# Pooled attention and a shrink MLP on one core: other PSUM banks for two pairs, one turn by DMA, the keys turned a block later, the last stores on two queues

## The chip, the core and the metric

The kernel runs on one core of a Trainium2 chip. The core has five engines that run side by side, each with its own in-order instruction stream: TensorE (PE, matrix products into PSUM), VectorE (DVE) and ScalarE (ACT) for element-wise work, GpSimd (POOL), and SyncE (SP), which here only issues DMAs. They meet through semaphores alone. The metric is the device time of one execution in microseconds (us); four executions of the kernel before gave a median of 294.24 us (293.37 to 294.52).

## The reference

Inputs are q, k and v of shape (8 batches, 8 heads, 576 tokens, 64), and two weight matrices.

```python
k_p = k.reshape(B, H, Sp, 8, D).mean(axis=3)          # 72 pooled keys a head
v_p = v.reshape(B, H, Sp, 8, D).mean(axis=3)
attn = softmax(q @ k_p.T / sqrt(D))
x = (attn @ v_p) -> (4608 tokens, 512)
h = x @ w_in                                          # 512 -> 2048
g = h - tanh(h)
out = g @ w_out                                       # 2048 -> 512, float32
```

## The kernel before, in words

**Two tilings overlap.** Attention works on batches of 576 tokens, in four blocks of 128 tokens and a fifth of 64 (block 4). The MLP works on nine groups of 512 tokens (TG = 512). Group 1, tokens 512 to 1023, thus needs block 4 of batch 0, blocks 0 to 2 of batch 1 and half of block 3 of batch 1. The rest of block 3 and block 4 of batch 1 belong to group 2. The attention result of a block lies in SBUF as x_sb (tokens on the partitions) and must be turned into xT (features on the partitions) before the MLP can use it. `x_pe_transpose` (lines 468 to 482) turns a block on PE: four matmuls with the identity into one PSUM bank, then one ACT copy into xT. `x_dma_transpose` (lines 457 to 466) turns it by a transposing DMA, issued by SP. The list `late` holds blocks that are turned by DMA once a group's pairs are done.

**Every order is written out by hand**, and each engine runs its instructions in the order of the program text. PSUM has eight banks of 128 x 512 floats, addressed by number. In the stretch that matters, `ps_any` hands out banks 5, 6, 7 in rotation, whatever asks for one. A bank that comes round again is free only when the engine that reads it has finished.

**The stretch around the change** is the output half of group 0 and the start of group 1. The loop over u = 0..15 runs `mlp_o` sixteen times, four matmuls of 512 columns each (line 540): quarter qd = u // 4 of the hidden units, token tile tb = u % 4. The four token tiles accumulate in banks 3, 4, 2 and 0, and are copied out to O in the last quarter (u = 12 to 15): tiles 0 and 2 by ACT, tiles 1 and 3 by DVE (line 549), and then stored by SP. Between these `mlp_o` calls stands the attention of batch 1: pooling of its keys (on POOL, lines 248 to 258), the turn of the keys (`k_transpose`, line 312; two banks, which DVE copies to KB at lines 302, 303 and 306), the turns of q (line 217, one bank each, copied by ACT), scores and their exponentials, and per block `av` (two banks, read by DVE, lines 415 and 416, into x_sb) with its turn (line 475, one bank, copied by ACT at line 482). Three banks per block, and three in the rotation: each turn uses the bank of the turn before it.

**Groups 1 to 8** run seven `h_pair`s and two `h_one`s (lines 558 to 576). A pair makes two hidden blocks in two neighbouring banks; ACT takes the tanh of both (line 570), DVE subtracts it (line 571) and thereby frees the banks. The bank list is (0, 2, 4, 6, 0, 2, 4), and the two ones use banks 0 and 1. In group 1 alone DVE also makes sums of weights (`w_sum`, line 597): two fp16 operands in SBUF, one sum after each of the first four pairs. Before the first pair it makes the larger sum `w_sum(b12, ...)`. At the same time POOL pools the values of batch 2 (`pool_v`, lines 269 to 293). Then come seven products per group (line 614), with the scores and `av` of the next batch in between. The last group is group 8; its last product is stored by ACT and SP (line 1026), after stores from SP and POOL (line 631).

Of the kernel before, what the change touches and what calls it, by code (L numbers as in the profile page):

```python
# [42 lines left out]
def kernel(  # L43
# [9 lines left out]
    nc = tc.nc  # L53
# [184 lines left out]
    def halves(n, b):  # L238
        return ((0, n),) if b < 2 else ((0, n // 2), (n // 2, n))

    def pool_k(b, eng, t0=0, t1=NT, mid=(), dep=None):
        r = k_raw[b % 2].rearrange("p t (j d) -> p t j d", d=D)[:, t0:t1, :, :]
        if b not in kdups:
            kdups[b] = work.tile([128, NT, 2, D], BF16, name="kd", tag="kd")
        kd = kdups[b][:, t0:t1, :, :]
        n = t1 - t0
        for ta, tb in halves(n, b):
            first = eng.tensor_tensor(  # L248
                out=r[:, ta:tb, 0:4, :], in0=r[:, ta:tb, 0:4, :], in1=r[:, ta:tb, 4:8, :], op=ALU.add
            )  # L250
            if dep is not None and ta == 0:
                after([first], dep)
        for c in mid:
            load_w2(c)
        eng.tensor_tensor(  # L255
            out=r[:, :, 0:2, :], in0=r[:, :, 0:2, :], in1=r[:, :, 2:4, :], op=ALU.add
        )
        eng.tensor_tensor(  # L258
            out=kd,
            in0=r[:, :, 0:1, :].to_broadcast([128, n, 2, D]),  # L260
            in1=r[:, :, 1:2, :].to_broadcast([128, n, 2, D]),
            op=ALU.add,
        )
        return first
# [158 lines left out]
    def new_x():  # L423
        return work.tile([128, 2, 4, D], BF16, name="x_sb", tag="x_sb", bufs=5)
# [16 lines left out]
    def av(b, blk, alloc, by_dma):  # L441
        x_sb = new_x()
        if by_dma:
            av_both(b, blk, x_sb)
        else:
            for half in range(2):
                av_half(b, blk, half, x_sb, alloc)
        if by_dma:
            if b * S + blk * 128 < (b + 1) * TG:
                x_dma_transpose(b, blk, x_sb)  # L450
            else:
                late.append((b, blk, x_sb))
        return x_sb

    late = []
# [78 lines left out]
    def mlp_o(g, tb, i0, i1, gts, pool=None):  # L534
        if i0 == 0:
            p, tag = pool or (ps_o, "o_ps")
            o_tiles[tb] = p.tile([128, DM], FP32, name="o_ps", tag=tag)
        o_ps = o_tiles[tb]
        for i in range(i0, i1):
            nc.tensor.matmul(  # L540
                o_ps[:, :],
                lhsT=gts[i][:, tb * 128 : (tb + 1) * 128],
                rhs=w2b[:, i, :],
                start=(i == 0),
                stop=(i == NHID - 1),
            )
        if i1 == NHID:
            o_sb = O[:, tb, :]
            (nc.vector.tensor_copy if g == 0 and tb % 2 else nc.scalar.copy)(
                out=o_sb, in_=o_ps[:, :]  # L550
            )
            for r0, r1, dst in out_segments(g * TG + tb * 128, 128):
                nc.sync.dma_start(out=dst, in_=o_sb[r0:r1, :])
# [12 lines left out]
    def h_pair(g, p, b0, ts):  # L566
        h_mms(g, p, PS[:, b0, :])
        h_mms(g, p + NP, PS[:, b0 + 1, :])
        t2 = TS[:, 2 * ts : 2 * ts + 2, :]
        nc.scalar.activation(out=t2, in_=PS[:, b0 : b0 + 2, :], func=ACT.Tanh)  # L570
        nc.vector.tensor_sub(out=Gt[:, p, :, :], in0=PS[:, b0 : b0 + 2, :], in1=t2)  # L571
# [129 lines left out]
    def after(lds, dep):  # L701
        for ld in lds:
            tc.add_manual_dep(
                ld.ins,
                dep.ins.name,
                mybir.DependencyInfo(mybir.DependencyClass.Sync, mybir.DependencyReason.DATA),
            )
# [212 lines left out]
    pend = []  # L920
    for u in range(16):
        qd, tb = u // 4, u % 4
        mlp_o(0, tb, qd * 4, qd * 4 + 4, gts, o_pools[tb])
        if u == 0:
            q_cast(1, nc.scalar.copy, 2)
            load_q(2)
        if u == 2:
            k_transpose(1, ps_any, (nc.vector.tensor_copy, nc.vector.tensor_copy))
        if u == 3:
            q_pe_transpose(1, (0, 1), "act")  # L930
        if u == 4:
            q_pe_transpose(1, (2,), "act")
            w_sum(w2s[:, 1, :, :], b11, b12, ALU.add)
            v1_done = pool_v(1, nc.vector)
            after(
                [
                    w_sum(w2s[:, 3, :, :], b21, b11, ALU.subtract, nc.gpsimd, k, k + 2)
                    for k in range(0, NP, 2)
                ],
                v1_done,  # L940
            )
        if u == 5:
            q_pe_transpose(1, (3,), "act")
        if 4 <= u <= 8:
            scores_wide(1, (u - 4,))
        if u == 6:
            q_pe_tail(1)
        if u == 8:
            scores_tail(1)
        if u in (9, 11):  # L950
            n = (u - 9) // 2
            nc.scalar.mul(
                out=w2s[:, 4, 4 * n : 4 * n + 4, :], in_=b22[:, 4 * n : 4 * n + 4, :], mul=-1.0
            )
        if u >= 9:
            if u >= 11 and pend:
                x_pe_transpose(1, *pend.pop(0))
            if u <= 13:
                pend.append((u - 9, av(1, u - 9, ps_any, False)))
    pool_k(2, nc.gpsimd)  # L960
    pool_v(2, nc.gpsimd)
    w_sum(b12, b22, b12, ALU.subtract)

    for g in range(1, NG):
        nb = g + 1 if g + 1 < B else None
        nn = g + 2 if g + 2 < B else None
        for p in range(NP - 1):
            c = p if g > 1 else p - 1
            if nb is not None and 0 <= c < 3:
                q_cast_part(nb, c)  # L970
            h_pair(g, p, (0, 2, 4, 6, 0, 2, 4)[p], p % 2)
            if g == 1 and p < 4:
                w_sum(w2s[:, 0, :, :], b11, b22, ALU.add, k0=2 * p, k1=2 * p + 2)
            if 3 <= p < 6:
                sum_p(2 * p - 6, 2 * p - 4)
            if nb is not None and p == 0:
                k_dma_transpose(nb)
            if g > 1 and p == 0:
                for tb in (2, 3, 0, 1):
                    store_tile(g - 1, tb)  # L980
            if nb is not None and p == 0:
                k_place(nb, nc.gpsimd.tensor_copy)
            if nb is not None and 0 <= c < 3:
                q_dma_transpose(nb, 2 * c, min(2 * c + 2, R + 1))
            if nb is not None and c == 2:
                if nn is not None:
                    load_k(nn)
                    load_v(nn)
                    load_q(nn)
        h_one(g, NP - 1, 1, 0, 2)  # L990
        h_one(g, NP - 1, 0, 1, 3)
        sum_p(6, 8)
        sum_q(0, 4)
        sum_q(4, 8)
        while late:
            x_dma_transpose(*late.pop(0))
        ps_a = Banks(2, 3, 4, 5, 0, 1)
        for u in range(14):
            n, half = u // 2, u % 2
            bk, lhs, rhs = products[n]  # L1000
            if n == 6 and g == NG - 1:
                break
            product(g, bk, lhs, rhs, 4 * half, 4 * half + 4, n < 2)
            if half:
                after_product(g, n)
                if g == 1 and n in (1, 2):
                    w_sum(w2s[:, 2, :, :], b21, b22, ALU.add, k0=4 * n - 4, k1=4 * n)
            if nb is not None:
                if u < NT:
                    scores(nb, u)  # L1010
                if u == NT:
                    ps_a.n += 2
                if u in (6, 7, 8, 9, 11):
                    av(nb, (6, 7, 8, 9, 11).index(u), ps_b1, True)
                if u == 6 and nn is not None:
                    pool_k(nn, nc.gpsimd, dep=gate[0])
                    pool_v(nn, nc.gpsimd)
        if g < NG - 1:
            nc.scalar.copy(out=O[:, 0:2, 0:HD], in_=chain(g, C1))  # L1019
    store(NG - 1, 1, (nc.sync, nc.gpsimd), HD, DM)  # L1020
    bk, lhs, rhs = products[6]
    for tt, eng in ((0, nc.scalar.copy), (1, nc.vector.tensor_copy)):
        product(NG - 1, bk, lhs, rhs, 0, NP, False, (tt,))
        eng(out=O[:, tt, 0:HD], in_=part(NG - 1, C1, tt))
        for n, (r0, r1, dst) in enumerate(out_segments((NG - 1) * TG + tt * 128, 128)):
            (nc.scalar if tt == 0 or n else nc.sync).dma_start(
                out=dst[:, 0:HD], in_=O[r0:r1, tt, 0:HD]
            )

# [29 lines left out]
```

## Time and profile before

| what | us |
|---|---|
| median of four runs | 294.24 |
| the profiled execution, whole | 294.93 |
| its span, first to last instruction | 293.2 |
| PE busy in the span | 278.6 |
| DVE busy in the span | 222.9 |
| PE idle before the key turn, at 37.18 | 0.59 |
| PE idle before group 1's first matmul, at 54.99 | 0.67 |
| PE idle before group 1's first single block, at 67.92 | 0.58 |
| PE idle at the starts of groups 3, 4, 5 | 0.92, 0.52, 0.76 |

The clock of PE was granted at 0.997 of full speed on average. Times in the text count from the start of the span. A line of the timeline gives start, duration, engine, source line, operation, output and inputs, their shapes, and in brackets how long the engine had been idle and what released it. An instruction's duration includes what it waits for after it was dispatched; POOL's are rough. The chain of waits is followed back from the last instruction, at each step to what released it.

### The profile page before, as it was taken

What the parts mean: (1) busy time and instruction counts of PE and PEld (TensorE: products, weight loads), DVE (VectorE), ACT (ScalarE), POOL (GpSimd) and SP (SyncE); (2) the same over time, 40 slices, a digit from 0 to 9 for tenths busy, and PEclk for the clock granted to TensorE, in tenths of its full rate; (3) what the DMA queues carried; (4) which work ended last, traced back from release to release, by engine and by line L of the source; (5) the groups of instructions that cost most, each with busy time, mean ns of one, the idle gap of its engine ahead of it and who ended that gap; (6) DMA issues with size and microseconds to landing.
All of it is one profiled execution on the core that took longest, in us unless ns stands there. A gap on an engine that the chain in (4) does not pass through costs nothing.

```text
span 293.2 us, 5365 instructions
## 1 busy us (share of the span) xinstructions
PE 278.6 (95%) x2021; PEld 178.6 (61%) x2040; DVE 222.9 (76%) x348; ACT 153.5 (52%) x243; POOL 135.1 (46%) x160
## 2 busy tenths in 40 slices
PE   7899999998999998999999998999999999999992
PEld 2454445444874587458845884489548944874681
DVE  6558665699995997599849983996799849927971
ACT  4637586585527652766176608660867046226510
POOL 8600818980099519920994099508960040030001
PEclk9999999999999999999999999999999999999998
DMA  7999999948827999489949993899492260021023
GB/s 252 224 213 280 303 207 331 306 79 255 239 55 105 261 338 130 113 245 299 122 99 262 342 110 77 230 330 158 66 201 45 56 171 2 0 76 69 0 57 90
DMA packets 64810, 49.84 MB, mean 170 GB/s; under 512 B 40048, under 2 KB 53744, under 8 KB 64784
## 3 DMA queue, kind: packets, MB, share of 16 engines
q1 hardware_dynamic: 54816, 35.40, 52.4%
q0 software_dynamic: 7312, 12.19, 18.5%
q10 hardware_dynamic: 2656, 1.90, 2.3%
q8 instruction: 16, 0.26, 0.4%
q14 instruction: 10, 0.08, 0.1%
HBM read 36.70 MB, written 9.44 MB: 157 GB/s over the span
## 4 chain that ended last, share of the span: by engine, by line
PE 72%; DMA 15%; DVE 6%; POOL 4%; issue 1%; ACT 1%; SPq 0%; POOLq 0%; DVEq 0%; ACTq 0%
PE PS L558 34%; PE PS L614 28%; DMA xT<-x_sb 7%; DMA w1b<-in_moe_w_in_dram 4%; PE PS L540 4%; DMA k_raw<-in_k_dram 4%; PE PS L398 3%; PE PS L351 3%; DVE Gt L571 3%; DVE w2s L597 1%; POOL k_raw L248 1%; DVE P L579 1%; POOL k_raw L255 1%; POOL kd L258 1%; POOL w2b L696 0%
## 5 line engine op out<-in xcount | busy, mean ns | idle before, releaser
L558 PE MATMUL PS<-xT,w1b 128*128 128x512 bf16 x496 | 111.1, 379 | 4.3 <-DMA xT<-x_sb 2.2
L571 DVE TENSOR_TENSOR Gt<-PS,TS 128x1024 bf16<-128x1024 f32 x56 | 68.3, 1220 | 31.5 <-ACT TS L570 31.5
L558 PEld LDWEIGHTS <-w1b 128*128 128x128 f16 x512 | 49.7, 98 | 63.2 <-issue 3.8
L570 ACT ACTIVATE TS<-PS 128x1024 f32<-128x1024 f32 x56 | 57.3, 1024 | 33.8 <-PE PS L558 27.1
L248 POOL TENSOR_TENSOR k_raw<-k_raw 128x512 f32<-128x512 f32 (+2 forms) x13 | 21.1, 1638 | 76.6 <-DVE rden L433 45.0
L635 POOL DMA_DIRECT2D out_dram<-O x44 | 23.7, 547 | 39.9 <-DVE O L673 22.3
L614 PE MATMUL PS<-w2s,Dg 128*128 128x256 f16 x256 | 30.2, 273 | 0.0
L614 PEld LDWEIGHTS <-Gt 128*128 128x128 bf16 x256 | 24.5, 98 | 5.7 <-DVE Gt L576 0.5
L614 PEld LDWEIGHTS <-P 128*128 128x128 bf16 x256 | 24.6, 98 | 4.7 <-issue 1.4
L614 PEld LDWEIGHTS <-Dg 128*128 128x128 bf16 x256 | 24.6, 98 | 2.6
L370 ACT ACTIVATE E<-PS 128x288 bf16<-128x288 f32 x60 | 21.4, 410 | 7.9 <-PE PS L351 7.6
L434 DVE TENSOR_TENSOR x_sb<-PS,rden 128x512 bf16<-128x512 f32 x30 | 20.7, 691 | 5.9 <-DMA xT<-x_sb 5.0
L579 DVE TENSOR_TENSOR P<-Gt 128x1024 bf16<-128x1024 bf16 x32 | 22.0, 686 | 0.6
L398 PE MATMUL PS<-VB,E 128*128 128x130 bf16 x240 | 20.2, 220 | 0.1
L670 ACT COPY m<-PS 128x512 f32<-128x512 f32 x8 | 4.7, 586 | 29.5 <-PE PS L614 29.5
L589 DVE TENSOR_TENSOR Dg<-Gt 128x1024 bf16<-128x1024 bf16 x32 | 19.9, 683 | 0.0
L269 POOL TENSOR_TENSOR v_raw<-v_raw 128x512 f32<-128x512 f32 (+1 forms) x12 | 19.6, 1653 | 0.0
L398 PEld LDWEIGHTS <-E 128*128 128x128 bf16 x240 | 16.8, 98 | 1.9 <-issue 0.4
L351 PE MATMUL PS<-qT,KB 128*128 128x288 bf16 (+5 forms) x128 | 17.0, 289 | 0.2
L614 PE MATMUL PS<-w2s,Gt 128*128 128x256 f16 x128 | 16.7, 273 | 0.4 <-DVE Gt L576 0.2
L1019 ACT COPY O<-PS 128x512 f32<-128x512 f32 x7 | 4.1, 585 | 24.5 <-PE PS L614 24.5
L614 PE MATMUL PS<-w2s,P 128*128 128x256 f16 x128 | 16.3, 273 | 0.0
(112 smaller groups left out, 387.7 us busy)
## 6 DMA issues: line engine op xcount, KB each, us to landing
k_raw<-in_k_dram SPq DMA_DIRECT2D x7, 1024.0 KB, 9.2
q_raw<-in_q_dram SPq DMA_DIRECT2D x7, 1024.0 KB, 11.9
v_raw<-in_v_dram SPq DMA_DIRECT2D x7, 1024.0 KB, 12.1
out_dram<-O POOLq DMA_DIRECT2D x32, 128.0 KB, 3.9
out_dram<-O POOLq DMA_DIRECT2D x12, 256.0 KB, 3.3
w1b<-in_moe_w_in_dram POOLq DMA_DIRECT2D x4, 512.0 KB, 14.1
w2b<-in_moe_w_out_dram POOLq DMA_DIRECT2D x4, 512.0 KB, 17.1
out_dram<-O SPq DMA_DIRECT2D x4, 256.0 KB, 4.6
```

The lines of the kernel that those rows point to most:

```text
L248: first = eng.tensor_tensor(out=r[:, ta:tb, 0:4, :], in0=r[:, ta:tb, 0:4, :], in1=r[:, ta:tb, 4:8, :], op=ALU.add)
L351: nc.tensor.matmul(dst[p : p + w], lhsT=KB[b % 2][:, o : o + w], rhs=qTs[b][:, m, c0:c1], start=True, stop=True,)
L370: nc.scalar.activation(out=E[:, t, half * hs : (half + 1) * hs], in_=ps[:, :], func=ACT.Exp, scale=SCALE)
L398: nc.tensor.matmul(ps[:, 2 * n : 2 * n + 2, :].rearrange("p h d -> p (h d)") if n < 2 else ps.rearrange("p (a s) d -> p a s d", s=2)[:, :, ...
L434: nc.vector.tensor_tensor(out=x_sb[:, :, :, :], in0=ps[:, :, :, 0:D], in1=rden[:, :, :, :].to_broadcast([128, 2, 4, D]), op=ALU.mult,)
L558: nc.tensor.matmul(dst, lhsT=w1b[:, fb, i * 128 : (i + 1) * 128], rhs=xT[:, fb, c0 : c0 + TG], start=(fb == 0), stop=(fb == NFB - 1),)
L570: nc.scalar.activation(out=t2, in_=PS[:, b0 : b0 + 2, :], func=ACT.Tanh)
L571: nc.vector.tensor_sub(out=Gt[:, p, :, :], in0=PS[:, b0 : b0 + 2, :], in1=t2)
L579: nc.vector.tensor_tensor(out=P[:, a:b, :], in0=Gt[:, a:b, 0, :], in1=Gt[:, a:b, 1, :], op=ALU.add)
L589: return nc.vector.tensor_tensor(out=Dg[:, a:b, :, :], in0=Gt[:, a:b, :, 0:HT], in1=Gt[:, a:b, :, HT:TG], op=ALU.subtract,)
L614: nc.tensor.matmul(part(g, bk, tt), lhsT=lhs(k, slice(tt * 128, (tt + 1) * 128)), rhs=rhs[:, k, :], start=(first and k == 0 and (tt == 0 o ...
L635: nc.gpsimd.dma_start(out=dst, in_=O[r0:r1, tb, :])
```

## The change

- `k_transpose` of batch 1 moves from behind `mlp_o` at u = 2 to behind `mlp_o` at u = 3, directly in front of the first two turns of q.
- The turn of block 3 of batch 1 moves from behind `mlp_o` at u = 14 to in front of it.
- The turn of block 4 of batch 1, behind `mlp_o` at u = 15, is taken away; the block goes to `late` and is turned by DMA at the end of group 1's pairs.
- In group 1, pair 0 uses banks 2 and 3 and pair 1 banks 0 and 1 (before: 0 and 1, then 2 and 3).
- In the last product of group 8, the first segment of both token tiles is stored by SP and the second by ACT. Before, ACT stored three and SP one.

```diff
     for u in range(16):
         qd, tb = u // 4, u % 4
+        if u == 14:
+            x_pe_transpose(1, *pend.pop(0))
         mlp_o(0, tb, qd * 4, qd * 4 + 4, gts, o_pools[tb])
...
-        if u == 2:
+        if u == 3:
             k_transpose(1, ps_any, (nc.vector.tensor_copy, nc.vector.tensor_copy))
-        if u == 3:
             q_pe_transpose(1, (0, 1), "act")
...
         if u >= 9:
-            if u >= 11 and pend:
+            if 11 <= u <= 13:
                 x_pe_transpose(1, *pend.pop(0))
             if u <= 13:
                 pend.append((u - 9, av(1, u - 9, ps_any, False)))
+    late.extend((1, blk, x_sb) for blk, x_sb in pend)
     pool_k(2, nc.gpsimd)
     pool_v(2, nc.gpsimd)
     w_sum(b12, b22, b12, ALU.subtract)
...
-            h_pair(g, p, (0, 2, 4, 6, 0, 2, 4)[p], p % 2)
+            h_pair(g, p, ((2, 0, 4, 6, 0, 2, 4) if g == 1 else (0, 2, 4, 6, 0, 2, 4))[p], p % 2)
...
         for n, (r0, r1, dst) in enumerate(out_segments((NG - 1) * TG + tt * 128, 128)):
-            (nc.scalar if tt == 0 or n else nc.sync).dma_start(
+            (nc.scalar if n else nc.sync).dma_start(
                 out=dst[:, 0:HD], in_=O[r0:r1, tt, 0:HD]
             )
```

## The prediction, made before the changed kernel was run

> **What bounds the kernel now.** I read the page first, then the chain of waits in order of time around 36 to 73 us, then the timeline there, engine by engine.
>
> ```profile
> PE 278.6 (95%) x2021; PEld 178.6 (61%) x2040; DVE 222.9 (76%) x348; ACT 153.5 (52%) x243; POOL 135.1 (46%) x160
> ```
>
> PE sets the time nearly everywhere, so what counts is where it stands. The chain:
>
> ```profile
> 36.18 1.54 POOL kd L258
> 37.77 0.45 PE PS L312 x5
> ...
> 54.01 0.88 PE PS L540 x4
> 54.91 0.70 DVE O L549
> 55.66 0.39 PE PS L558
> ...
> 59.94 1.64 DVE w2s L597
> 61.58 1.13 DVE Gt L571
> ```
>
> Three things: PE waits for POOL before the key turn; it waits for DVE's copy out of bank 0 before group 1's first pair; and from 58.7 us to about 72 us the chain runs on DVE, not PE. So a gain of PE at 55 us counts only if DVE can use it.
>
> **Part 1, the keys a block later.** Windows of PE and DVE:
>
> ```profile
> 37.77 0.45 PE L312 MATMUL PS<-ident,kd 128*128 128x128 bf16 x5 [0.59 <-POOL kd L258]
> ...
> 38.28 0.45 DVE L302 CAST KB<-PS 64x288 bf16<-64x288 f32 x1 [2.33 <-PE PS L312]
> 38.74 0.40 DVE L303 CAST KB<-PS 64x224 bf16<-64x224 f32 x1
> ```
>
> The last matmul of `mlp_o` at u = 2 ends at 37.18; as one of 0.38 us is followed 0.22 after its start by the next, PE could issue again at 37.02. The keys came at 37.72. Now `mlp_o` at u = 3 runs first, 0.86 us (the chain's rows of four), to 37.88, and the turn starts there without a wait: 0.11 later than before. Behind it now stand two turns of q, with nothing between. Keys take two banks, the first q turn the third, and the second q turn comes round to the first: it must wait until DVE has copied KB, at 38.74 + 0.40 + 0.11 = 39.25 us, while PE is through with the keys (0.28) and the first q turn (0.22) at 38.38. So a wait of about 0.9 takes the place of one of 0.75. The next `mlp_o` starts near 39.52 against 39.41: a **loss of 0.11 us** on PE, passed on to 52 us, since PE stands nowhere for over 0.12 us between. Were the bank free, the 0.9 would be gone and the edit would gain 0.8; I take the loss, as the rotation is in the code. Behind the waiting q turn on PE stand `mlp_o` and the first score; DVE's next sum ends 0.11 later, hidden by its 0.43 of idle time before the values.
>
> **Part 2, turns and banks at u = 14 and 15.**
>
> ```profile
> 52.61 0.59 ACT L482 CAST xT<-PS 128x512 bf16<-128x512 f32 x1 [0.58 <-PE PS L475]
> ...
> 52.76 1.03 PE L540 MATMUL PS<-w2b,Gt 128*128 128x512 f16 x4
> ...
> 53.82 0.59 ACT L549 COPY O<-PS 128x512 f32<-128x512 f32 x1 [0.63 <-PE PS L540]
> ```
>
> The turn of block 3, now in front of `mlp_o` at u = 14, needs the bank of block 2's turn, which ACT copies until 53.20, shifted to 53.31. PE would have been there at 52.76 + 0.11: it stands about 0.48, turns (0.22) until 53.57, runs both `mlp_o`s (0.86 each) until 55.30. Block 4's turn (0.12 on PE, 0.37 on ACT) is gone. Pair 0 now needs bank 2, freed by ACT's copy of tile 2: start 53.57 + 1.06 (52.76 to 53.82), plus 0.59 and 0.05 for the semaphore, 55.27. So group 1 starts near 55.30, not 55.66: **0.36 us earlier**, part 1 included. Bounds: -0.2 (if ACT, which now copies block 3's turn ahead of tile 2, falls a copy of 0.59 behind) to 0.85 (no wait at block 3). Pair 1 needs bank 0, which DVE frees near 56.2, before it is due at 57.0. Pair 4 now waits for pair 1's subtraction instead of pair 0's; PE wants that bank at 62.2, and it ends at 61.4 by part 3: nothing.
>
> **Part 3, DVE against POOL.** Single instructions of the two:
>
> ```profile
> 58.71 1.22 DVE L571 TENSOR_TENSOR Gt<-PS,TS 128x1024 bf16<-128x1024 f32 x1 [1.94 <-ACT TS L570]
> 59.85 1.72 DVE L597 TENSOR_TENSOR w2s<-w2b 128x512 f16<-128x512 f16 x1
> ...
> 57.85 1.82 POOL L269 TENSOR_TENSOR v_raw<-v_raw 128x768 f32<-128x768 f32 x1
> 59.75 1.55 POOL L272 TENSOR_TENSOR v_raw<-v_raw 128x640 f32<-128x640 f32 x1
> ...
> 62.64 1.07 DVE L597 TENSOR_TENSOR w2s<-w2b 128x512 f16<-128x512 f16 x1
> ...
> 66.30 0.41 DVE L597 TENSOR_TENSOR w2s<-w2b 128x512 f16<-128x512 f16 x1
> ...
> 62.38 1.05 POOL L283 TENSOR_TENSOR VB<-v_raw,mask 128x512 bf16<-128x512 f32 x1
> ```
>
> The same sum takes 0.41, 1.07 or 1.72 us. Both long ones end 0.28 us after the POOL instruction that ran when they were ready (L272 ends 61.30, sum 61.58; L283 ends 63.43, sum 63.70): such a sum waits for the POOL instruction that is under way, then goes ahead of POOL's next. The first was ready at 59.94 and missed the gap between L269 (ends 59.67) and L272 (59.75) by 0.2 us. POOL's place hangs on DMAs, not on PE. With the pair 0.36 earlier it is ready near 59.58, while L269 runs, and should slip in at its end.
>
> The Trainium skill (SBUF — State Buffer, "SBUF: two separate sides") says that a DVE instruction with two SBUF inputs and a reading GpSimd instruction share a port pair as a lock, held by whichever starts first for the whole instruction. Read so, the sum wins if issued ahead of L272 and part 3 is worth 0.9 us; issued behind it, nothing.
>
> L269's end must be redone: the large sum of DVE (1.25 us) now is ready at 56.19, not 55.6, behind L269's first half (55.7 to 56.9); it runs to 58.0, and the second half (1.78 from the port's release) ends at 59.78. The sum ends at 60.06. Tanh of pair 1, behind pair 0's tanh and a cast (1.02, 1.04, 1.02, from 57.30), is done at 60.18: ACT is next. Subtraction 1 starts near 60.2 (before 61.50), 2 near 62.1 (63.63), 3 near 64.0 (65.17; its sum waits for L283), 4 near 66.4 (67.23; the sums wait for the KB copies of 0.4 and less). POOL stops then, and what is left is **0.7 to 1.0 us; I take 0.9**. PE then leads to the end of the group, and later groups hang on their own order, DMAs included, so it carries on. Bounds: 0 (the gap is missed) to 2.0 (the four sums took 3.68 us, four at 0.41 take 1.64).
>
> **Part 4, block 4 by DMA.** SP issues it behind the last q load at 72.5, after waiting for a key load that has landed; it reads a buffer that is ready and next needed at 86 us. In this trace xT's DMA turns land 2.3 to 9.7 us after issue, so by 82.3, and group 2 starts at 86.4. SP's next turn is due at 81.2, and an issue here takes 1.2 to 3.9. Cover of some 4 us: **nothing**; uncovered, 1.2 of SP's issue in front of group 2's turns.
>
> The Trainium skill (VectorE: DVE Perf Modes, "The three transpose paths") speaks against this edit: 390 ns for a turn on TensorE, 1309 ns by DMA. On the path it would cost 0.9 us; the rows above keep it off.
>
> **Part 5, the last stores.**
>
> ```profile
> 287.06 2.34 ACTq L1026 DMA_DIRECT2D out_dram<-O  x3
> ...
> L1054 POOLq DRAIN  x3: 46/102/5201, 287.2 to 292.9; - x3
> ```
>
> ACT's third issue starts at 288.63 and lands at 290.98; now it can start when DVE's copy ends, near 288.0: 0.6 earlier. SP is free at 287.65 and issues its two by 288.6. But SP is through with all DMA waits at 291.38, while POOL's DRAIN runs to 292.39 and the closing barrier follows it. POOL's stores don't move. So **0**, and 0.6 at best (if the drain waits for these stores); a loss of 0.1 if SP's second issue becomes last.
>
> **Sum.** -0.9 on the profiled execution's 294.93 (span 293.2): 294.0. That execution lies 0.69 above the median; the same step from 294.24 gives **293.3**.
>
> **Rivals.**
> - *The gap is missed* (294.2). If PE gains under 0.1 us at group 1's start, or L269 ends earlier than 59.6, the sum waits for L272 again, and PE's gain is swallowed by POOL. For it: only 0.2 us of margin, and POOL rows are rough. Against: the rows of part 2 add to 0.36.
> - *POOL keeps the port* (slower, 295.7). Place: 56.9 us, where the large sum, now late, meets L269's two halves back to back. If POOL's queued instruction went first, and L272 after it, the sum would run from 60.2 to 61.4 and subtraction 0 end at 62.6, not 59.94; the first small sum then meets L275 to L293 and subtraction 1 starts at 63 to 64, against 61.5. With the 0.7 that later sums then save, some +1.5 us. It decides at two POOL instructions in a row; one alone costs nothing. Against: at 63.43 the waiting sum went ahead of a queued one.
> - *The end counts too* (292.7): part 5 gives 0.6 on top. For it: SP's last wait does end with ACT's last store. Against: the DRAIN's 5.2 us.
>
> **How the numbers follow.** Forecast 0.52, gap missed 0.25, POOL keeps the port 0.13, end counts 0.10. The forecast alone spans 292.6 to 293.8. The range takes in the end case in part and the missed gap with its noise, and leaves most of the slower case out: 292.4 to 294.9. A measurement of this kernel can tell 0.3% (0.88 us) from no change. Faster: 0.35 of the forecast and the end case, 0.45. Slower: the port case and 0.04 of the missed gap, 0.17. Same: the rest, 0.38.
>
> **What would show it.** Right: no PE wait on kd, but one of 0.9 before the second q turn; one of 0.5 before block 3's turn; pair 0 near 55.3; a first small sum of about 0.5 us; L272 starting behind it. Wrong: a first small sum that ends after L272, a large sum over 2 us, or a group 2 that waits for xT.

## The result, and the profile after

| | before | after |
|---|---|---|
| median of all runs, us | 294.40 (63 runs) | 293.66 (44 runs) |
| after / before | | 0.996, 95% interval 0.9944 to 0.9976 |
| profiled execution, us | 294.93 | 292.05 |
| its span, us | 293.2 | 290.3 |

The changed kernel is faster by 0.4%: 0.996 of the 294.24 from which the forecast was made is 293.1, and 293.3 was forecast. The ratio leaves out slow executions, which either kernel has (3 of the 44 after the change); the medians of all runs stand 0.25% apart. Twelve of the 44 executions are faster than the fastest of the 63 before (292.95). Single executions of either kernel lie some 3 us apart, and the two profiled ones differ by more than the ratio says. Below, the place of an event in a trace tells what happened, and the ratio of many runs what it is worth.

The first part of the changed kernel's page, busy time of each engine:

```profile
PE 278.1 (96%) x2017; PEld 178.7 (62%) x2036; DVE 221.6 (76%) x348; ACT 153.2 (53%) x242; POOL 135.4 (47%) x160
```

PE lost 0.5 us of work (four matmuls of block 4's turn among it), far less than the span lost. The time came out of waits. First the timeline of the changed kernel, PE and DVE, at the keys and in front of group 1:

```profile
37.84 0.44 PE L312 MATMUL PS<-ident,kd 128*128 128x128 bf16 x5
...
38.80 0.40 DVE L303 CAST KB<-PS 64x224 bf16<-64x224 f32 x1
39.25 0.22 PE L217 MATMUL PS<-ident,q_bf 128*128 128x128 bf16 x1 [0.74 <-DVE KB L303]
...
53.30 0.38 PE L475 MATMUL PS<-ident,x_sb 128*128 128x128 bf16 x4 [0.32 <-ACT xT L482]
...
55.24 0.81 PE L558 MATMUL PS<-xT,w1b 128*128 128x512 bf16 x2
```

The wait on kd is gone, and in its place PE stands 0.74 us before the second q turn, until DVE has copied the keys out of that bank. It stands again before block 3's turn, for ACT's copy of block 2. Group 1's first pair no longer waits: it starts at 55.24, against 55.66 with 0.67 of idle time before it.

Now DVE and POOL of the same timeline:

```profile
56.05 1.80 DVE L597 TENSOR_TENSOR w2b<-w2b 128x2048 f16<-128x2048 f16 x1
...
59.43 0.41 DVE L597 TENSOR_TENSOR w2s<-w2b 128x512 f16<-128x512 f16 x1
60.15 1.23 DVE L571 TENSOR_TENSOR Gt<-PS,TS 128x1024 bf16<-128x1024 f32 x1 [0.30 <-ACT TS L570]
...
59.60 1.65 POOL L272 TENSOR_TENSOR v_raw<-v_raw 128x640 f32<-128x640 f32 x1
```

Before, the first small sum came 0.10 behind POOL's L272 and lasted 1.72. Here it comes 0.17 ahead of it and lasts 0.41; subtraction 1 stands at 60.15 instead of 61.50, and what releases it is ACT's tanh, no longer DVE. The seventh subtraction starts at 69.52 (before 70.82), group 2 at 85.25 (86.40), group 3 at 115.47 (116.71). The chain of waits of the changed kernel shows who leads now:

```profile
58.15 1.04 ACT q_bf L192
59.19 0.37 ACT TS L570
59.56 0.44 issue
60.01 1.04 ACT q_bf L192
61.05 0.93 ACT TS L570
61.98 0.02 issue
62.01 1.22 DVE Gt L571
```

Where the chain before had DVE's sum at 59.94, ACT's q casts and tanh now stand, up to subtraction 2 at 62.01: ACT is the next limit in the first pairs. From there the chain runs on DVE again.

Behind group 3 the two traces part further. The kernel before waits at the starts of groups 4 and 5 for xT's DMA turns:

```profile
146.61 2.75 PE L558 MATMUL PS<-xT,w1b 128*128 128x512 bf16 x11 [0.52 <-DMA xT<-x_sb]
176.75 2.53 PE L558 MATMUL PS<-xT,w1b 128*128 128x512 bf16 x10 [0.76 <-DMA xT<-x_sb]
```

The changed kernel doesn't wait in these two places:

```profile
144.69 4.48 PE L558 MATMUL PS<-xT,w1b 128*128 128x512 bf16 x19
173.91 5.34 PE L558 MATMUL PS<-xT,w1b 128*128 128x512 bf16 x23
```

So the lead grows from 1.24 at group 3 to 1.92 at group 4 and 2.84 at group 5, and PE's last matmul starts at 284.39 against 287.22. More than half of the difference between the two traces arises behind group 2, away from the edited stretch.

### The profile page after: what moved, and what is told of

It is laid out like the page before. It is cut to its first block, busy times and chain, and to the rows that moved or that the text cites. A ratio compares the mean times of both kernels' runs of the same rounds, so it can differ in the third digit from the quotient of the medians.

```text
span 290.3 us, 5359 instructions
## 1 busy us (share of the span) xinstructions
PE 278.1 (96%) x2017; PEld 178.7 (62%) x2036; DVE 221.6 (76%) x348; ACT 153.2 (53%) x242; POOL 135.4 (47%) x160
## 3 DMA queue, kind: packets, MB, share of 16 engines
q10 hardware_dynamic: 2576, 1.84, 2.3%
## 4 chain that ended last, share of the span: by engine, by line
PE 84%; DVE 6%; DMA 3%; ACT 3%; issue 1%; SPq 0%; ACTq 0%; DVEq 0%
PE PS L558 34%; PE PS L614 33%; PE PS L540 5%; PE PS L398 4%; PE PS L351 4%; PE PS L512 2%; DMA k_raw<-in_k_dram 2%; DVE Gt L571 2%; DVE Gt L525 2%; DMA xT<-x_sb 1%; ACT q_bf L192 1%; DVE P L579 1%; ACT TS L570 0%; PE PS L475 0%; PE PS L800 0%
## 5 line engine op out<-in xcount | busy, mean ns | idle before, releaser
L558 PEld LDWEIGHTS <-w1b 128*128 128x128 f16 x512 | 50.0, 98 | 60.2 <-issue 1.4
L579 DVE TENSOR_TENSOR P<-Gt 128x1024 bf16<-128x1024 bf16 x32 | 22.2, 695 | 0.6
L269 POOL TENSOR_TENSOR v_raw<-v_raw 128x512 f32<-128x512 f32 (+1 forms) x12 | 19.2, 1619 | 0.0
```

The lines of the kernel that those rows point to most:

```text
L558: nc.tensor.matmul(dst, lhsT=w1b[:, fb, i * 128 : (i + 1) * 128], rhs=xT[:, fb, c0 : c0 + TG], start=(fb == 0), stop=(fb == NFB - 1),)
L579: nc.vector.tensor_tensor(out=P[:, a:b, :], in0=Gt[:, a:b, 0, :], in1=Gt[:, a:b, 1, :], op=ALU.add)
```

## The experiments

Twelve kernels, one of them the changed kernel unaltered, ran in three groups, each group on one chip with runs of the kernel before (medians 294.56, 294.78, 294.80). The gap is the moment between the end of POOL's L269 and the start of its L272: a small sum that starts before L272 does "wins" it. A "margin" below is the start of L272 less the start of the first small sum: positive, the sum was first. "Pairs" is the time from group 1's first matmul to the start of its seventh subtraction.

| kernel | group 1 | margin | first sum lasts | pairs | group 2 | group 3 | ratio (95%) |
|---|---|---|---|---|---|---|---|
| before | 55.66 | -0.10 | 1.72 | 15.16 | 86.40 | 116.71 | |
| after | 55.24 | +0.17 | 0.41 | 14.28 | 85.25 | 115.47 | 0.996 (0.9944 to 0.9976) |
| keys edit alone | 55.74 | -0.30 | 1.53 | 14.98 | 86.32 | 116.71 | 1.0031 (1.0002 to 1.0060) |
| banks alone | 54.70 | +0.34 | 0.55 | 14.27 | 84.56 | 115.96 | 1.0015 (0.9980 to 1.0050) |
| before, sums late | 55.99 | none | 0.41 | 14.40 | 86.31 | 116.65 | 0.9982 (0.9948 to 1.0016) |
| after, old banks | 56.16 | -0.60 | 1.23 | 14.67 | 86.45 | 117.28 | 1.0004 (0.9968 to 1.0040) |
| after, one matmul more | 55.48 | +0.14 | 0.41 | 14.28 | 85.37 | 115.45 | 0.9974 (0.9936 to 1.0013) |
| after, two more | 55.46 | +0.01 | 0.41 | 14.28 | 85.34 | 115.67 | 0.9962 (0.9920 to 1.0004) |
| after, q turns apart | 54.32 | +0.96 | 1.17 | 14.87 | 84.80 | 114.94 | 0.9899 (0.9859 to 0.9939) |
| that, old place of block 3, sums late | 54.49 | none | 0.67 | 14.82 | 85.25 | 117.12 | 0.9947 (0.9912 to 0.9981) |
| after, once more | 55.50 | -0.07 | 1.75 | 15.19 | 86.31 | 117.47 | 0.9951 (0.9927 to 0.9974) |
| q turns apart, old place of block 3 | 54.96 | +0.96 | 1.16 | 14.86 | 85.45 | 115.25 | 0.9917 (0.9889 to 0.9944) |
| after, block 4 on PE | 55.54 | -0.26 | 1.57 | 14.99 | 86.12 | 116.52 | 0.9991 (0.9964 to 1.0018) |
| after, old last stores | 56.97 | -0.13 | 1.69 | 15.12 | 87.70 | 117.93 | 0.9953 (0.9929 to 0.9978) |

There is one trace of each, and the part ahead of the change already differs between them. PE's first matmul of L475 starts at 31.65 to 32.47, but at 33.77 with the old last stores, where PE is thus some 1.5 late; POOL's keys (L258) end at 37.07 to 38.13, but at 38.58 in the kernel with the q turns apart and block 3 in its old place, 0.9 later than before. This shifts PE's starts as a whole. Pairs don't have that shift in them; starts do, and a margin moves with PE's shift against POOL's.

What follows behind group 2 differs as well: from its start to the start of PE's last matmul it takes 200.82 us before, 199.14 after, and 198.73 to 201.30 in the other traces (203.13 with the small sums moved). That is more than the 0.9 by which pairs differ, and no experiment here holds it fixed.

**The keys edit alone.** The kernel before, with

```diff
-        if u == 2:
+        if u == 3:
             k_transpose(1, ps_any, (nc.vector.tensor_copy, nc.vector.tensor_copy))
-        if u == 3:
             q_pe_transpose(1, (0, 1), "act")
```

> The kernel before, with the keys' turn moved behind u = 3 and nothing else. My theory (the wait on kd gives way to a wait for the bank of the keys): PE's wait on kd (0.59 us before) is gone, a wait of 0.7 to 0.9 us stands before the second turn of q, group 1 starts near 55.7 us (before 55.66), its first small sum still takes some 1.7 us behind a POOL instruction, group 2 starts near 86.4 and the time is that of before within 0.1%. Rival (the wait on kd was worth its 0.59): group 1 starts near 55.1, the small sum falls into the gap, group 2 starts near 85.2, time -0.4%.

PE waits 0.74 before the second q turn and not on kd, and group 1 starts 0.08 later than before. The sum misses the gap by more, and the ratio lies just above 1, where no more than 0.1% of change was expected. This edit trades one wait for another of its length and brings nothing.

**The banks alone.** The kernel before, with

```diff
-            h_pair(g, p, (0, 2, 4, 6, 0, 2, 4)[p], p % 2)
+            h_pair(g, p, ((2, 0, 4, 6, 0, 2, 4) if g == 1 else (0, 2, 4, 6, 0, 2, 4))[p], p % 2)
```

> The kernel before, with banks 2 and 3 for group 1's first pair, 0 and 1 for its second, and nothing else. My theory (one term carries the gain: the pair no longer waits for DVE's copy out of bank 0, and the first small sum then falls into the gap between two POOL instructions): group 1 starts at 54.9 to 55.0 (it then waits for ACT's copy of block 3's turn, which ended at 54.90), even before the changed kernel's 55.24; the small sum is ready near 59.25 and done near 59.95; group 2 starts at 85.2 to 85.4 and the time is that of the changed kernel, ratio 0.996 to the kernel before. Rival (the parts are needed together): less than half of that, group 2 at 85.9 or later.

The trace has all of the change's gain and more: group 1 at 54.70 without the other waits, the first sum ahead of L272, group 2 1.84 us earlier than before (0.25 of it from keys that ended earlier in this run). By group 3 most of that is gone, as this line of its timeline shows:

```profile
115.96 2.32 PE L558 MATMUL PS<-xT,w1b 128*128 128x512 bf16 x10 [2.01 <-DMA xT<-x_sb]
```

Group 3 waits for the DMA turns of batch 3 (the kernel before waits 0.92 here, the changed one 0.83), which stand in SP's queue behind the loads of batch 4. That takes 1.1 of the 1.84, and 0.75 is left. At group 5 PE waits 0.82 for such turns, where the kernel before waits 0.76. The twelve timed runs (292.86 to 297.07) show no gain at all, so a won gap in this trace didn't bring the change's time. Why stays open.

**The small sums moved away from POOL.** The kernel before, with

```diff
-            if g == 1 and p < 4:
-                w_sum(w2s[:, 0, :, :], b11, b22, ALU.add, k0=2 * p, k1=2 * p + 2)
+            if g == 1 and p >= 3:
+                w_sum(w2s[:, 0, :, :], b11, b22, ALU.add, k0=2 * p - 6, k1=2 * p - 4)
```

> The kernel before, with group 1's four small sums behind pairs 3 to 6 instead of 0 to 3, when POOL has little left to do, and nothing else. PE's start of group 1 stays at 55.66. Theory that POOL's hold of the port is what costs: the four sums take near 0.41 each (1.6 to 1.9 in all, before 3.68), the second subtraction starts near 60.6 instead of 61.50, and group 2 starts at 85.1 to 85.5 (before 86.40), ratio near 0.996. Rival (PE's start of group 1 is what counts): group 2 stays at 86.4, ratio 1.000.

From its timeline, DVE, beside the lines of before in the prediction:

```profile
64.17 1.23 DVE L571 TENSOR_TENSOR Gt<-PS,TS 128x1024 bf16<-128x1024 f32 x1 [0.18 <-ACT TS L570]
65.31 0.41 DVE L597 TENSOR_TENSOR w2s<-w2b 128x512 f16<-128x512 f16 x1
...
66.25 1.22 DVE L571 TENSOR_TENSOR Gt<-PS,TS 128x1024 bf16<-128x1024 f32 x1
```

The traced execution took 297.11, 3 us above the median of its twelve, so only its group 1 is read here. Every sum now takes 0.41, and subtractions 1 to 3 start at 60.91, 62.76 and 64.17 (before 61.50, 63.63, 65.17), though PE began 0.33 later: POOL's hold did sit in these pairs. But a sum, L579 (another sum that DVE makes behind pairs 3 to 5) and a subtraction then fill DVE, 2.07 us a pair, and the seventh subtraction stands only 0.43 earlier. PE waits 0.54 for L576, the subtraction of a single block, in front of the products. More than half of the gain of 1.00 at subtraction 3 is given back, and the ratio isn't told from 1.

**The change with the old banks.** The changed kernel, with

```diff
-            h_pair(g, p, ((2, 0, 4, 6, 0, 2, 4) if g == 1 else (0, 2, 4, 6, 0, 2, 4))[p], p % 2)
+            h_pair(g, p, (0, 2, 4, 6, 0, 2, 4)[p], p % 2)
```

> The changed kernel with the old banks for group 1's pairs. The first pair waits for DVE's copy out of bank 0, which in the changed kernel ends at 56.14: it starts near 56.2, later than in the kernel before (55.66). By the theory of the gap the first small sum is ready near 60.45, behind the start of POOL's instruction at 59.6, and ends near 61.4; group 2 starts at 86.2 to 86.5, ratio to the kernel before 0.999 to 1.002. By the rival that the moved turns and keys bring the gain: group 2 stays near 85.3, ratio 0.996.

PE, DVE and POOL of its timeline:

```profile
56.16 1.04 PE L558 MATMUL PS<-xT,w1b 128*128 128x512 bf16 x4 [0.79 <-DVE O L549]
...
60.36 1.23 DVE L597 TENSOR_TENSOR w2s<-w2b 128x512 f16<-128x512 f16 x1
...
59.76 1.55 POOL L272 TENSOR_TENSOR v_raw<-v_raw 128x640 f32<-128x640 f32 x1
```

PE waits 0.79 for DVE's copy out of bank 0, group 1 starts at 56.16, the sum is 0.60 behind L272, and the ratio is 1.0004. Without the banks no gain of the change is seen, though the two intervals overlap a little. Together with the banks alone, the banks are needed but not shown to be enough.

**PE made later, in two doses.** The changed kernel, with one or two idle matmuls in front of group 1's first pair:

```diff
+            if g == 1 and p == 0:
+                for _ in range(1):
+                    nc.tensor.matmul(
+                        bank(1, [128, TG]), lhsT=ident[:, :], rhs=w1b[:, 0, 0:TG], start=True, stop=True
+                    )
```

> The changed kernel with one matmul of 512 columns more (0.22 us) in front of group 1's first pair, into a bank that is free then; the output is the same. Theory of the gap: the small sum is ready near 59.73, some 0.1 us behind the start of POOL's instruction (59.6 in the changed kernel's trace), ends near 61.4 instead of 59.85, and group 2 starts 0.8 to 1.2 later, at 86.1 to 86.4. Rival (PE's delay passes through as it is): group 2 starts 0.22 later, at 85.5.

> The same with two such matmuls (0.43 us). Theory of the gap: the small sum is ready near 59.95 and still ends near 61.4, so group 2 starts where it does with one more matmul, at 86.1 to 86.4: a step, not a slope, ratio to the kernel before near 1.000. Rival (passes through): group 2 at 85.7, ratio 0.997 to 0.998.

The dose was meant to push the sum behind L272. It didn't get there: POOL was later in both runs, and PE's early part earlier in the second. But the second shows how fine the edge is:

```profile
58.50 1.23 DVE L571 TENSOR_TENSOR Gt<-PS,TS 128x1024 bf16<-128x1024 f32 x1 [0.61 <-ACT TS L570]
59.64 0.41 DVE L597 TENSOR_TENSOR w2s<-w2b 128x512 f16<-128x512 f16 x1
...
59.65 1.81 POOL L272 TENSOR_TENSOR v_raw<-v_raw 128x640 f32<-128x640 f32 x1
```

The sum was dispatched 10 ns ahead of L272, while the subtraction before it still ran (until 59.73), and took its 0.41; L272 took 1.81 instead of 1.55. So here the order of dispatch decided, and being first on a busy engine was enough. A start 0.24 later than the changed kernel's, with the gap still won, costs 0.12 at group 2; whether a lost gap costs a whole step was left to the repetition below.

**The q turns set apart.** The changed kernel, with the second q turn behind `mlp_o` at u = 4, so that it doesn't wait for the keys' bank:

```diff
         if u == 3:
             k_transpose(1, ps_any, (nc.vector.tensor_copy, nc.vector.tensor_copy))
-            q_pe_transpose(1, (0, 1), "act")
+            q_pe_transpose(1, (0,), "act")
         if u == 4:
-            q_pe_transpose(1, (2,), "act")
+            q_pe_transpose(1, (1, 2), "act")
```

> The changed kernel with the second turn of q behind the mlp_o of u = 4, so that the keys' banks are long free when it comes. PE's wait of 0.74 before that turn goes, and group 1 starts near 54.5 (changed kernel 55.24). Theory of the gap: no gain from it, since the small sum, ready near 58.8, waits for the end of POOL's L269 near 59.6 and ends near 59.9; group 2 starts at 85.1 to 85.4, time as the changed kernel's within 0.1%. Rival (passes through): group 2 near 84.5, time 0.25% below the changed kernel's.

PE's timeline and the first sum:

```profile
38.06 0.39 PE L217 MATMUL PS<-ident,q_bf 128*128 128x128 bf16 x4
38.28 1.03 PE L540 MATMUL PS<-w2b,Gt 128*128 128x512 f16 x4
...
58.51 1.17 DVE L597 TENSOR_TENSOR w2s<-w2b 128x512 f16<-128x512 f16 x1
```

The 0.74 is gone and group 1 starts at 54.32. The sum now comes so early (58.51) that it waits for L269's end at 59.39 and ends 0.3 behind it. The expectation took that for the end of all gain. It isn't: tanh and q casts on ACT, the limit in the changed kernel's first pairs, run 0.9 earlier too, so subtraction 1 follows the sum at 59.60, where it had waited for ACT until 60.15. What leads in these pairs is then DVE, with the sum that L269's end releases. Group 2 starts 0.45 earlier than in the changed kernel. The ratio, 0.9899, is the lowest of all, and its interval ends just below the changed kernel's (from 0.9944), though the two were not measured on one chip. It stands for 3.0 us (1.8 to 4.2), while group 2 is 1.60 earlier than before; the trace, which waits 0.75 at group 5 and took 292.69, doesn't show where the rest comes from.

**Everything early.** The last kernel with block 3's turn back behind `mlp_o` at u = 14, and the small sums at pairs 3 to 6:

```diff
-        if u == 14:
-            x_pe_transpose(1, *pend.pop(0))
...
-            if 11 <= u <= 13:
+            if 11 <= u <= 14:
...
-            if g == 1 and p < 4:
-                w_sum(w2s[:, 0, :, :], b11, b22, ALU.add, k0=2 * p, k1=2 * p + 2)
+            if g == 1 and p >= 3:
+                w_sum(w2s[:, 0, :, :], b11, b22, ALU.add, k0=2 * p - 6, k1=2 * p - 4)
```

> The changed kernel with the second turn of q behind u = 4's mlp_o, block 3's turn between the last two mlp_o (as before the change), and the four small sums behind pairs 3 to 6. If both limits are real (PE's start and POOL's port), they go together here: group 1 starts at 54.2 to 54.4, no small sum waits for more than one short POOL copy, ACT's tanh and casts lead the first pairs, and group 2 starts at 84.2 to 84.8; ratio to the kernel before 0.992 to 0.995. Rival (something else on DVE or ACT leads by then): group 2 no earlier than 85.2, ratio 0.996.

Subtractions 1 and 2 come early (59.39, 61.25), the late sums give it back, and group 2 starts at 85.25, as the rival had it. Group 3 then waits 2.50 for xT's DMA turns. At 0.9947 it is no better than the change.

**The changed kernel once more**, unaltered, on the chip of the three runs after it.

> The changed kernel once more, beside the next three on one chip, since runs of one kernel lie 3 us apart and earlier ratios came from different chips. Theory: ratio to the kernel before 0.994 to 0.998; group 1's pairs take 14.2 to 14.4 us from PE's start to the seventh subtraction (15.16 in the kernel before), because the first small sum goes ahead of POOL's instruction. Rival (the first trace was a lucky one): 15 us, and ratio 1.000.

```profile
59.69 1.75 DVE L597 TENSOR_TENSOR w2s<-w2b 128x512 f16<-128x512 f16 x1
...
59.62 1.54 POOL L272 TENSOR_TENSOR v_raw<-v_raw 128x640 f32<-128x640 f32 x1
```

The same program, and here the sum missed the gap, by 0.07. PE was 0.26 later than in the first trace (group 1 at 55.50 against 55.24), POOL's L272 only 0.02, and that is more than the margin of 0.17. The pairs take 15.19, as before the change, against 14.28 in the other trace: a lost gap costs 0.9, and nothing in between was seen at this edge. So of two traced executions one won and one lost. The trace is as the rival had it, and yet the ratio of the twelve runs, 0.9951, is the theory's.

**The apart version with block 3's old place**, but the sums left where they are (the first two hunks of "everything early").

> The changed kernel with the second turn of q behind u = 4's mlp_o (as in e8) and block 3's turn back between the last two mlp_o: both new waits of PE (0.74 and 0.32) are taken away, the small sums stay where they are. PE starts group 1 near 54.0. If POOL's end of L269 (near 59.5) sets the first small sum, group 2 starts where it did in e8, 84.6 to 84.9, and the time is e8's, ratio 0.990 to 0.994. Rival (PE's start passes through): group 2 near 84.2.

This trace has its early part 0.9 late, yet group 2 stands at 85.45 and the span is 290.1. The ratio is 0.9917, from six runs (291.47 to 293.02), beside 0.9951 for the changed kernel on the same chip, with intervals that just overlap. Its sum was 0.96 ahead of L272, which is more than any shift of PE against POOL between these traces.

**Block 4 turned on PE again.** The changed kernel, with

```diff
-            if 11 <= u <= 13:
+            if 11 <= u <= 13 or u == 15:
```

> The changed kernel with block 4 turned on PE again, behind the mlp_o of u = 15. Theory (the DMA turn costs nothing, the PE turn 0.12 us): group 1 starts near 55.37 instead of 55.24, SP has one transposing DMA less, group 2 starts within 0.2 of the changed kernel's 85.25 as long as the small sum is still issued ahead of POOL's instruction (margin 0.17 in its trace), ratio to the changed kernel within 0.1%. Rival (the block's move to DMA is what frees PE and ACT): group 2 near 86.2.

The turn puts 0.12 on PE in front of group 1 (55.42 to 55.54), the sum is 0.26 behind L272, and the ratio is 0.9991. The expected 0.1% to the changed kernel is missed, though the intervals overlap a little. A PE turn of 0.12 can't by itself be the 1.2 us between 0.9991 and 0.9951. That it turns a gap won in some executions into one that is lost in nearly all fits both, but this trace doesn't show it: PE was 0.18 later than in the changed kernel's first trace ahead of the turn, and L272 0.13 earlier, so the gap would have been lost without the turn.

**The old last stores.** The changed kernel, with

```diff
-            (nc.scalar if n else nc.sync).dma_start(
+            (nc.scalar if tt == 0 or n else nc.sync).dma_start(
```

> The changed kernel with the last stores as before, three from ACT and one from SP. Theory: POOL's DRAIN of 5.2 us sets the end, so from PE's last matmul to the end of the span it takes 5.94 us as in all traces so far, and the time is the changed kernel's. Rival (ACT's third store counts): 6.3 to 6.6 us, time 0.15 to 0.2% longer.

0.9953, beside 0.9951 with the new stores. From the instructions of the end, the changed kernel first:

```profile
L1056 POOLq DRAIN  x3: 46/93/5201, 284.4 to 290.1; - x3
```

and the kernel with the old stores:

```profile
L1056 POOLq DRAIN  x3: 46/93/5204, 286.8 to 292.5; - x3
```

The columns are shortest, median and longest in ns. POOL's closing DRAIN takes 5.2 us either way, and from PE's last matmul to the end of the span it is 5.94 to 5.96 in every trace of the study. No effect of the stores is seen.

## Why the prediction was right

**The keys.** Forecast: the wait on kd replaced by one of 0.9, 0.11 lost. Measured: 0.74 shown (0.91 counted as the forecast counts, from when PE could issue again at 38.34), 39.25 for the second q turn as worked out, and `mlp_o` at 39.47 against 39.41, so 0.06 lost. The edit alone moved group 1's start by 0.08 and the ratio to 1.0031. Right, the remark that a free bank would make it a gain of 0.8 included: setting the q turns apart moved group 1 by 0.92.

**Turns and banks.** Forecast: a wait of 0.48 before block 3's turn and the pair at 55.30. Measured: 0.32 idle, 0.49 from issue to issue, and 55.24. Right. The old banks put 0.79 of waiting back, and no gain was left in the timed runs.

**DVE and POOL.** Forecast: the large sum behind L269's first half, the first small sum in the gap, subtraction 1 near 60.2, the next near 62.1 and 64.0, gain 0.7 to 1.0. Measured: the large sum lasted 1.80 instead of 1.25, and the subtractions start at 60.15, 62.01 and 63.75. The fourth small sum took no longer than 0.48 and the third 0.67, so subtraction 4 came at 65.93 and not 66.4. So the gain was taken somewhat too small: group 2 is 1.15 earlier in the trace, or 0.96 when both are counted from the end of POOL's keys (37.71 before, 37.52 after), where 0.9 was taken. One detail was wrong: the sum was to wait for L269's end until 60.06; it started at 59.43 with L269 over at 59.53, and took no longer than its 0.41.

**The missed gap** was a rival at 0.25, and it isn't false: it happens, in one of the changed kernel's two traces. There the first small sum ends at 61.44, after L272 (61.16), which the prediction had named as a sign of being wrong. The forecast treated as one outcome what changes from one execution to the next. The profiled executions side with it at first sight: won gaps, in the changed kernel and the two with idle matmuls, took 292.05, 292.28 and 292.29 us; lost ones, in the changed kernel repeated, with block 4 on PE and with the old stores, 294.22, 293.87 and 294.60. Yet the banks alone won it and took 293.51, and the last three all carry other delays: the repeated one and the one with block 4 on PE take 1.1 and 0.9 more behind group 2 than the changed kernel's first trace, and with the old stores PE was 1.5 late from the start. The timed runs, which have no trace, can't be sorted by the gap. How often it is won, and so how much of the 0.4% it carries, stays open.

**POOL keeps the port**, the slower rival, was not borne out. The large sum did meet L269's two halves back to back, and got in behind the first: 56.05 to 57.85, ending well before subtraction 0 was due at 58.29.

**Block 4 by DMA.** Forecast: nothing. Its turn was issued at 72.25 and had landed by 81.74, with group 2 at 85.25 and no wait there: the cover held. It isn't quite nothing to put it back, since the 0.12 on PE comes out of a margin of 0.17. The Trainium skill (VectorE: DVE Perf Modes, "The three transpose paths") has the DMA turn as the dearer one, 1309 ns against 390 for a 128x128 turn. Here, behind loads in the same queue, this one took 9.49 us from issue to landing, and PE still didn't wait for it.

**The last stores**, forecast at 0, measured 0.9953 against 0.9951; the rival that the end counts was not borne out, as the tail is 5.94 to 5.96 with and without them.

**It carries on**, said of the gain behind group 1, held in this trace up to group 3 (1.15 at group 2, 1.24 at group 3), but not as a rule: banks alone lost 1.1 of its 1.84 to the xT turns at group 3. And it isn't all: by PE's last matmul the lead of this trace is 2.83, for the waits at groups 4 and 5 are gone, which the forecast had no term for.

So the stretch of code went as forecast in the first trace, term by term. That the timed 1.2 us (0.4%) lies near the forecast 0.9 is in part luck: the gap was won in one of two traced executions, and what happens behind group 2 moves the time by as much.

## What to carry to other kernels

Before moving an instruction, follow the PSUM bank that it will be handed: a turn moved next to another that shares a rotating bank trades one wait for the next (0.75 for 0.74 here), and one `mlp_o` put between them took it away. Where DVE and POOL meet on SBUF, ask not only how long each takes but which is dispatched first, and whether the lead is larger than what moves it from run to run; the lead of 0.17 us here was there in one traced execution and gone in the next. And after a stall is taken away, look who releases the next instruction: here it was ACT, and the next gain came from what made ACT earlier. Last, follow the gain to the end of the program before trusting it: here waits for DMA turns in the next groups gave or took as much as the edit.

## What the runs showed of the hardware

- **Dispatch order decides the port; in one trace 10 ns were enough.** In all traces where the small sum and L272 met, the one with the earlier start went first: sum first by 0.01, 0.14, 0.17 and 0.34 us, 0.41 to 0.55 for it; sum later by 0.07 to 0.60, and it took 1.23 to 1.75, ending 0.3 us or less behind L272. The Trainium skill (SBUF — State Buffer, "Who interferes with whom") says that issue order and not the kind of operation decides who blocks; these rows agree, and the one with 0.01 adds that the start counts even while the engine still works on the instruction before.
- **A waiting DVE instruction gets in between two queued POOL instructions.** The large sum (56.05) and, with the q turns apart, the first small sum (58.51) both waited for the POOL instruction under way and went ahead of the next. What POOL pays for the large sum is the same whichever half of L269 it holds up. Before, the sum started ahead of the first half; after, behind it (shortest, median and longest in ns):

```profile
L269 POOL TENSOR_TENSOR v_raw<-v_raw x2: 1817/2030/2244, 55.6 to 57.9; 128x512 f32<-128x512 f32 x1, 128x768 f32<-128x768 f32 x1
```

```profile
L269 POOL TENSOR_TENSOR v_raw<-v_raw x2: 1262/2030/2797, 55.5 to 56.7; 128x512 f32<-128x512 f32 x1, 128x768 f32<-128x768 f32 x1
```

  Held up, the first half takes 2.24 instead of 1.26, or the second 2.80 instead of 1.82: 0.98 either way, and 4.01 to 4.04 us for both in every trace.
- **The end is POOL's DRAIN**, 5201 to 5206 ns in every trace, and the tail of 5.94 to 5.96 us from PE's last matmul doesn't move with which queue stores last.
